# A Fourier convolution beside an FFN: the last inverse stage as even and odd parts in time

## The chip, the cores and the metric

The kernel runs on one core of a Trainium2 chip. The metric is the time that the device takes for one execution, in microseconds, as the median of several runs. The engines that matter are TensorE (PE in the profile, with its weight loads as PEld), VectorE (DVE), ScalarE (ACT), GpSimd (POOL), and SyncE (SP), which issues most of the DMAs. ACT issues a few DMAs too.

## The reference

The output is a token plus the product of two branches, both fed by the layer norm of the token: a state space layer, which is a causal convolution over time with a kernel of 2048 taps for each of 512 channels, and the SiLU of a SwiGLU feed-forward network (FFN).

```python
def _A_ref(u, A_re, A_im, B_re, B_im, C_re, C_im, log_dt, Dskip):      # L, D, N = 2048, 512, 128
    dt = jnp.exp(log_dt)[:, None]
    logdA, dB = dt * (A_re + 1j * A_im), dt * (B_re + 1j * B_im)
    P = jnp.exp(logdA[:, :, None] * l[None, None, :])
    K = jnp.einsum("dn,dnl,dn->dl", C_re + 1j * C_im, P, dB).real      # the 2048 taps
    ...                                # zero padding to 2L, rfft of K and u, product, irfft, first L
    return y + u * Dskip
def _B_ref(x, w_gate, w_up, w_down):                                   # F = 1792
    return (_silu(x @ w_gate) * (x @ w_up)) @ w_down

x = A_u                                                                # (1, 2048, 512), f32
xn = _layernorm(x, axis=-1)
return x + _A_ref(xn, ...) * _silu(_B_ref(xn, B_w_gate, B_w_up, B_w_down))
```

## The kernel before

Time is cut as 64 x 32: t = 32 t1 + t2. The 16 token tiles (j = 0 to 15) hold 128 tokens each: the 64 rows t1 of column t2 = 16 + j in the upper half of the partitions and those of its mirror 16 - j in the lower half (`rows`). Two neighbouring tiles make one of the eight blocks b of the FFN, each of which is worked in seven chunks c of its width: 24 matmuls for the gate, 24 for the up weights (line 717, called a half unit each below), and the down product (760; 769 for the last tile, in two halves of the channels). All weights and activations of the FFN are split into a high and a low f16 part, and three products of the parts are summed.

The convolution is a Fourier transform in two stages each way. The first stage on the tokens (`x_stage1`, line 568) transforms over t1: for each tile, six f16 matmuls of 64 rows by 128 columns, one for either half, in two row groups of the PE array at a time. ACT and DVE form the sum and the difference of the two halves and SP writes them to `ax_d` in DRAM. The taps are computed and transformed by `kg_tables` to `kg_s1` (lines 1106 to 1229) and go to `ak_d`. The second stage (`s2_mm`, 1267 for the taps and 1275 for the tokens) transforms over t2, `s2_prod` multiplies, and `s2_inv` (1320, with an ACT copy at 1330 and a DVE add and subtract at 1328 and 1329) goes back over the first digit of the frequency and writes `bs_d`. This is done for two halves of the channels, c = 0 and 1, of 256 each.

`final` does the last inverse stage. For a pair of tiles and a half of the channels (14 units; the last two tiles are done one by one over all channels, line 1372) it loads 512 KB of `bs_d` into `bt`, and four f32 matmuls (line 1365) take the 128 rows, real and imaginary parts of 64 frequencies, to 64 values of time: a 128x64 table for 16 + j and one for 16 - j, side by side in two column groups. DVE multiplies by the gate `zgs` (or by what was stored in `zg_d` and loaded again) at 1393, POOL or DVE adds the token (1396, 1398), which is loaded once more (1351), and the result is stored (1400; 1384 for the last tiles), one half by SP and one by ACT.

The kernel is written as tasks with an engine, buffers and dependences. Their order is a list written out as numbers (`LIST`), the place of each SBUF buffer another (`PLACES`); PSUM banks (eight, `p`) are given out in that order. `Plan.run` replays the list with priced durations only to choose the banks and to find gaps of PE that are filled with idle matmuls (line 1487). Each engine works its queue in order, and so does SP with its DMAs.

Of the kernel before, what the change touches and what calls it, by code (L numbers as in the profile page):

```python
# [26 lines left out]
NC = 7  # L27
# [11 lines left out]
BN = 2 * P + 6  # L39
# [7 lines left out]
    "###&#%#)#'#(#*#L#P#M#Q#S#N#+#l#O#K#W#X#$#J#`#g#I#Z#A#n#o#H#_#b#a#,#m#R#p#Y#/#h#|#i#q#U#c#[#B&0#]&2#.#^&5#V#T#t#v"  # L47
    "#j#u#{#r#D&A&6#w(2(3#9#s#}#d&B#k#x#2(4(5#y$#$$&1$,#5#e&;#f$%(7(8(9&<#@$'(6$|$}$&#1$+$-#E$((:(;(<(D(F&C&D#4$6$)$."
    "$/%##7%$%+(E(G$2&3$7(J(L(=$8%,$9#8%<#;$A&H(>(K$:$B$C$D#3$0$1$;&E(?(@#F$E&7$F$3&J$H(P#0$*#=$W$I&9&=&>(H&@$M$G(i#:"
    "$L&8$5$4%=%>$=(Q(V(W(X$N$O(A#-#z#?&F$b(M$J#>$P(B%%$Q#6$<(R&M&4(k$X(Y(c$S$T(C$p(I(d$R(Z(o&G%*%3$Y%4&:$>$?%&$K(S(j"  # L50
    "(l%'$Z$[(p(q(r&I&P$U%7$]#<(m(u$@$V$c&N(T$^({(|(v&K([%(%-&L%)%0(w$_$d&Q(x#C%?%@(U$g(]$e&_(_$f(^$`%.(n%5&R),(`(y$a"
    "$q%/&O%2$m$h(z%1%F%G$r$i%H$n$o%I$j)&)()')-))(a(b&i%8$k(s$l(}%J)#)$%A%B&S%9).)*)+)2)3):)%);$s$t$y(e)G)H)I)P%K%L%M"
    "$z${$u)Q%N&j$v$w$x)R%C&T&U&V&W%6%D%O&`&a&k%Q&s&t%E)S&u%R%P)<)=-Y)D-Z-_%:(N)T(f(g(t(O)E(h&b)>)?%;%S%T)F)J&w&?)K)U"
    "&x&y&m&n&v&o&q&p&z&X&Y&Z-`&c)]&d&e&f&l)^)L-[&[&^&r-]-a-^-o-v-s&{&])@)l)s)t)M)A-w)_)u)`&g)B)/)0)v&|)1-q-r)N)g)O.0"
    ".7-b)C.8-p-t-y-u-d-f-e-x-i&h-z.$-j-c-h)}*#*$*%.#.')h)i-k)j#G)k)V)X-l.1.:.H.G)W.I.J-g-m-n.*.+)Y.9.;.,-{..)Z)[.%.&"
    ".).--|)m.K.L)4.2.3.(-}.5)o.M.N.4.6.O.P)n.U.V)p.W.Y.X./.<.=.>)6.[.R)5.e)q)r.Q.x.].^)7)a.k)b)8.l.T.`.S.c)9)c.y/5.d"
    ".g)w/6/7._*;)d*<.f)x.b.a.Z.h)e.r.s)f.t.v/4.?.B.u.A.@.C.D.E/&)y/$/(*&*'*.*//%/'.m)z%U.z/8.o.q*=*D.n.p.w.|/#.{.}%V"
    ".i.F/9/:/;/B%]%^%s%t.j/)/</**E*L/+*>){)|/,%n%o%p/0%u*M*N///-/./1%[*0/?*O/A/=*1*8/2*9*:%q%r/D/I/F/>/@/C/E/3*?*@*A"
    "/H%e%f/L/Q/S%v%w&.*B/W/J/K'%*F*G*2*4%Z*3*5/N/M/O'$*H&}*I/_%X/e/n%W*C/P*(**/G*)/R/T*6/X%Y%_'+%`%b*7%a*+*,/Y/U*P*Q"
    "*R%c%x%i*-*V*W/V/[/^*J*K/f*S*_*`')/`/l%d/}/Z/]0#/a/b*T%y*r/m'('-*a/|*c'M0$/c*U'9/g/h*b%z/i%{%|*X/o0%/p0&0'/j'&/d"  # L60
    "/k/q/r*d'''#'**Z*e'/*Y','.*g'0'C/s/t*f/u*[*]%}&#&$&('1'2*^%g':';'<0D*y'N/w/v%j%k'D/x/y%h&,*z'E'O/z&%&)+&*h*o*p'3"
    "'4/{'='>'G'H'?'A'Q'R&&+''@%l*q+.&*'5'7%m050<'6&+&'0M'I'J'S'T0=060?&/+/+0&-'8+10>0708090(0@01*s'L*i*t'K0;0:0*0+0)"
    "*u0i0R0Q0-*v'U0/00020j0E*j0n0,0.030o0p'V+2+3+4*k0K0L0X0Y+5+6+70H040l0A0F0J0[0k0m0q0r0G0N+(+*0B*l0O0Z*{*m0C0I0]+)"
    "'Y0s0S0U0t*}0P*n0T0V++0W'Z0u0^*w*x+8+9*|+#+,+-0}'a0{1&0x0|0z1#0v0w1$+$+%0y+S+Z+[1(1)0_151*1'1-1B0`1<1C1.'o+:1=1/"
    "+c101+11+;1,0a0d1%12160b0c0e0f0g191;1?1718+@1Z0h1[1]'X1Y1>1:+<+=1F1H+d1314+A1^1_1`1@+B+D1I+>+?+k1J1L1D1E1G1A1K1M"
    "1N+C+E1a+F1e1h1i'['W'`'e'B']'b1b+H+I'^+G+l1j'P1c1d'_'c'd+P'p((()'F+T1g1o+Q+R1f1k(*1O1P+m1}1l+n'q'y'z'{(,1Q1U(-+U"
    "(.1m(/(11n1T's'f'g(0't'u'w'v'x1u1v1w20+V+W1R1S1V1p+o1q2#1W1x1s1y1r1t+p+q1X+r2+2-+X+Y2&2/2G2F+J1z1{2('}1|(#($(&(%"
    "(''i+L'j'k'l+K28'n+M2H+]2$2%2''m212)2:2*2,2223252I+_+^+`+s+t262729+a+N2J2K2L2M2O2P+b2Q24+O2T+e+f2N2R2S+g+h2U2W2Z"
    "2b2_2.2;2V2<2X2[+u2=2a+i+v2j2c2e(+2d2f2]2^2`+w+x+y2n+j2Y2k2s2u2w2p2l2m2o2g2q7a2{2h2x3#3$4T+z3&2r'|2y2z34352t364/"
    "2}3%333'374.2|+},#,$,&,%'r'h,*3839,'+{2i+|,(,)2>2?2A2B2@2C7b2v3(3:4-3)3*40414243453;3{3}3|47,+4#4$464%44,4484&4)"  # L70
    "2E,;,<4'4(2D493+3>4*4,3@4G3/3,4+3.3-303C3E7O,=3A,>3B3D3<3=,C3?7N4:4A4D4E4>4q4?4V,D,K,23F32313G3N3O,L4B3V4F4;4<3H"
    "3K3P3R4@,,3M3I3J3L3Q,33W4C3^3_3a,53`3b3Z3X3Y3[3]4|3S5#3d3m,-3e,.,63o3k3h4=5H3j3T3U3f4I4W3l3n3g3i4X4Y,M,74U4Z,/,8"
    ",94^4[4]4_3c3p3q3r,0,14a4J4L4K4o4r4t4H4s4p5J3s5K,:3u3t3v5=5M5$3w3x4M4P5I4}4`5%4Q5&4O4N4R,?,@5N5L5O,N4S7k,A5R5;3z"
    ",B3y5<,O7j5Q5P7|4u4v4x4w,E4y4z5'5+5(,F4b5S4c5*4l5)694{5,5-5>6.,T4d4m4e4i4f4g,U6-5@5A5?4j4k5E5D5B,]5C5.554n585652"
    "53,G,H5/504h5o546x,I5T5F6:595:,P,J515G5U5V,Q,R5W5X,S6;,^,_5]5^5_5`5a5b5Y6=6>5Z6<6?,`6A6@5q5s6z6{5r6|6/6B,e6D6C7}"
    "62,a5[606163655p5t646668675u5x5w5v5y5z,V6y6}7#7&7$,X7%8I,W,Y,b575d6E6S7(6F6G7*,Z6I6J6O5c,o,v,c,[,d6R6L,w5e5f5g6P"
    "6T6U6V7)6M7',f6H7+7,5h5k5l5i6K-#5j5m,m5n7Y6W6Z-$-+6X6Y7P7-7.6_7V6N7Z6[6Q6^6]7X7M70717/727473-%-&867[,n7W5{6$6*6%"
    "7{5|5}6`7`7]7^6a6c6b6+7r6#6'6(6),g,h7Q7R7S8R7U6d6e,x7_6f6h6g75797:6&7?7@7u7v7T7i-,-.8d8c7<7=7>7677--7;6j6i6k6u6o"
    "6v7A,z7G85,i8Q-/,y8.6l7w,{78,|6,7t6r7D7s,j,k,p,r-'6p7x7E6m6s,q,s6n,t,l-46w6t,u6q8m7C-5-67y,}-7-8-9878X8[8^7d7m7F"
    "-:-;8)8b8e8g8#7B7H8=8H8]8F8k8O8G-(8f-)-*8?-08+8z8n-<-=->-@-1-28%8h8*7I7J8$-3848&8(-?-A-B8o8l8/80888i8,8Z898:8S8T"  # L80
    "8p-C8Y8_8-817z8P8j9#7c8J8A8@8K8L8>8U8a8'7l-D-E-F8|7L-J8N-L-N-P-R8y8;-G-T7e7f-I7h-V8q8r828s8t-K8M8{837g8B8C8D-H8W"
    "8<8E7n7o7p8V-M-O8u8v-Q8x-X9(9)-S9*9+-U-W8`8}9$7q8w7K9%9&9'"
# [298 lines left out]
def kernel(  # L381
# [24 lines left out]
    bs_d = dram.tile([2, 16, BN, HD], F32, name="bs_d")  # L406
# [1128 lines left out]
```

## Time and profile before

| | us |
|---|---|
| median of 3 runs (lowest, highest) | 577.08 (577.01, 577.15) |
| the profiled execution | 578.55 |
| its span, first to last instruction | 576.8 |
| PE busy | 565.2 (98%) |
| DVE, ACT, POOL busy | 440.9, 334.7, 327.1 |
| matmuls of the FFN, lines 717, 760, 769, busy | 309.1, 143.2, 9.3 |
| line 1365, line 568, busy | 13.9, 11.9 |

Rows of the profile name line, engine, operation, written and read tiles, partitions x elements, and the number of records. An f32 matmul leaves two. "<-" behind an idle time names what released the engine. SPq and ACTq are the two queues of issued DMAs; their times are those of the issue. Busy times of matmuls overlap, so a sum of them is more than the stream's length; the chain's pieces don't overlap.

### The profile page before, as it was taken

What the parts mean: (1) busy time and instruction counts of PE and PEld (TensorE: products, weight loads), DVE (VectorE), ACT (ScalarE), POOL (GpSimd) and SP (SyncE); (2) the same over time, 40 slices, a digit from 0 to 9 for tenths busy, and PEclk for the clock granted to TensorE, in tenths of its full rate; (3) what the DMA queues carried; (4) which work ended last, traced back from release to release, by engine and by line L of the source; (5) the groups of instructions that cost most, each with busy time, mean ns of one, the idle gap of its engine ahead of it and who ended that gap; (6) DMA issues with size and microseconds to landing.
All of it is one profiled execution on the core that took longest, in us unless ns stands there. A gap on an engine that the chain in (4) does not pass through costs nothing.

```text
span 576.8 us, 18270 instructions
## 1 busy us (share of the span) xinstructions
PE 565.2 (98%) x7570; PEld 405.9 (70%) x7570; DVE 440.9 (76%) x1006; ACT 334.7 (58%) x686; POOL 327.1 (57%) x301
## 2 busy tenths in 40 slices
PE   7999999999999999999999999999999999999996
PEld 3788896564886588757867688765766674678765
DVE  5988889846788998988887899977978765643533
ACT  5988667646767266777777778746752323231111
POOL 0144352299998168629998789997516152520041
PEclk9999999999999999999999999999999999999999
DMA  8888722251003171058005452697879987998997
GB/s 249 237 260 265 225 74 74 49 174 67 29 2 85 29 174 47 2 110 275 22 1 126 97 149 74 149 212 181 270 230 248 287 281 218 258 306 234 233 256 203
DMA packets 113155, 93.17 MB, mean 162 GB/s; under 512 B 51184, under 2 KB 97648, under 8 KB 113072
## 3 DMA queue, kind: packets, MB, share of 16 engines
q1 hardware_dynamic: 110432, 89.61, 55.5%
q10 hardware_dynamic: 2640, 2.39, 1.5%
q8 instruction: 59, 0.97, 0.7%
q14 instruction: 24, 0.20, 0.1%
HBM read 55.94 MB, written 32.90 MB: 154 GB/s over the span
## 4 chain that ended last, share of the span: by engine, by line
PE 93%; DMA 2%; SPq 2%; DVE 1%; issue 1%; ACT 0%; DVEq 0%
PE p L717 50%; PE p L760 24%; PE p L1181 5%; PE p L1267 3%; PE p L568 2%; PE p L1275 2%; PE p L1365 2%; PE p L1320 2%; PE p L769 2%; PE p L1214 2%; DMA arena<-bs_d 1%; DMA arena<-in_A_u_dram 1%; SPq L464 1%; PE p L830 1%; SPq L485 1%
## 5 line engine op out<-in xcount | busy, mean ns | idle before, releaser
L717 PE MATMUL p<-arena,wu 128*128 128x256 f16 x1344 | 154.6, 273 | 0.0
L717 PE MATMUL p<-arena,wg 128*128 128x256 f16 x1344 | 154.5, 273 | 0.0
L717 PEld LDWEIGHTS <-wg 128*128 128x128 f16 x1344 | 130.5, 98 | 21.4 <-issue 2.8
L717 PEld LDWEIGHTS <-wu 128*128 128x128 f16 x1344 | 130.2, 98 | 20.2 <-issue 3.7
L760 PE MATMUL p<-wd,arena 128*128 128x512 f16 x630 | 143.2, 379 | 0.0
L760 PEld LDWEIGHTS <-arena 128*128 128x128 f16 x630 | 59.7, 98 | 71.8 <-issue 6.1
L1114 POOL TENSOR_TENSOR arena<-arena 128x1536 f32<-128x1536 f32 x32 | 90.6, 2839 | 22.0 <-DVE arena L850 8.3
L739 ACT ACTIVATE arena<-p,inv 128x512 f32<-128x512 f32 x56 | 37.7, 685 | 65.9 <-PE p L717 62.5
L741 DVE SCALAR_TENSOR_TENSOR p<-p,shc,arena 128x512 f32<-128x512 f32 x56 | 42.0, 756 | 41.9 <-PE p L717 33.3
L1106 POOL TENSOR_TENSOR arena<-arena 128x1024 int32<-128x1024 int32 x32 | 62.4, 1955 | 20.0 <-DVE arena L532 7.8
L743 ACT CAST arena<-p 128x512 f16<-128x512 f32 x56 | 32.6, 586 | 38.4 <-DVE p L741 31.9
L1149 DVE TENSOR_TENSOR arena<-arena,p 128x512 f32<-128x512 f32 x64 | 43.6, 681 | 6.3 <-POOL arena L1047 2.5
L1129 ACT ACTIVATE p<-arena 128x512 f32<-128x512 int32 x64 | 38.5, 606 | 12.9 <-POOL arena L1106 8.3
L1396 POOL TENSOR_TENSOR arena<-arena 128x512 f32<-128x512 f32 x12 | 15.0, 1269 | 49.3 <-DMA arena<-in_A_u_dram 21.6
L1130 ACT ACTIVATE p<-p,halfpi 128x512 f32<-128x512 f32 x64 | 41.9, 662 | 1.2
L744 DVE TENSOR_TENSOR arena<-p,arena 128x512 f16<-128x512 f32 x56 | 37.5, 683 | 6.0 <-ACT arena L743 5.9
L1131 ACT ACTIVATE p<-arena 128x512 f32<-128x512 int32 x64 | 38.0, 604 | 6.9 <-POOL arena L1106 4.2
L1298 POOL TENSOR_TENSOR arena<-arena 128x512 f32<-128x512 f32 x16 | 20.3, 1274 | 30.7 <-DVE arena L1295 26.2
L1297 POOL TENSOR_TENSOR arena<-arena 128x512 f32<-128x512 f32 x16 | 20.4, 1276 | 25.4 <-issue 15.0
L1181 PEld LDWEIGHTS p<-arena 128*32 128x32 f32 x2048 | 29.4, 110 | 5.4 <-issue 2.9
L1181 PE MATMUL p<-arena 128*32 128x64 f32 x2048 | 32.3, 220 | 0.0
L1293 DVE TENSOR_TENSOR arena<-p,arena 128x512 f32<-128x512 f32 x32 | 21.1, 685 | 13.9 <-PE p L1275 7.7
(198 smaller groups left out, 815.5 us busy)
## 6 DMA issues: line engine op xcount, KB each, us to landing
ax_d<-arena SPq DMA_DIRECT2D x32, 256.0 KB, 2.9
ak_d<-arena SPq DMA_DIRECT2D x16, 512.0 KB, 5.6
arena<-ak_d SPq DMA_DIRECT2D x16, 512.0 KB, 4.6
arena<-ax_d SPq DMA_DIRECT2D x16, 512.0 KB, 5.1
bs_d<-arena SPq DMA_DIRECT2D x32, 256.0 KB, 3.8
arena<-in_A_u_dram SPq DMA_DIRECT2D x62, 128.0 KB, 3.9
arena<-in_B_w_down_dram SPq DMA_DIRECT2D x14, 512.0 KB, 5.1
arena<-bs_d SPq DMA_DIRECT2D x12, 512.0 KB, 6.7
```

The source lines that it names most:

```text
L717: T.matmul(pg.t[:, i * 256:(i + 1) * 256].rearrange("p (a t) -> p a t", a=2), w[:, wl, d, i * P:(i + 1) * P], x[:, :, xl, d, :], start=(k ...
L739: add("ACT", 0.69, lambda: S.activation(sg.f32(), pg.t, AF.Silu, scale=inv[:, c, 0:1]), rd=[pg], wr=[sg], c=1, pr=e)
L741: add("DVE", 0.75, lambda: V.scalar_tensor_tensor(pu.t, pu.t, shc[:, c:c + 1], sg.f32(), op0=ALU.mult, op1=ALU.mult), rd=[sg], wr=[pu], c= ...
L744: add("DVE", 0.7, lambda: V.tensor_tensor(hh.view(F16)[:, 512:1024], pu.t, hh.view(F16)[:, 0:512], op=ALU.subtract), rd=[pu], wr=[hh], c=1 ...
L760: T.matmul(z.t, h[:, hl, i * 256 + t * P:i * 256 + (t + 1) * P], w[:, wl, i], start=(c == 0 and i == 0 and k == 0), stop=(c == NC - 1 and ...
L1106: G.tensor_tensor(a, h_[:, :, :, None].to_broadcast([P, 2 * GT, 4, 8]), l_[:, :, None, :].to_broadcast([P, 2 * GT, 4, 8]), op=ALU.add)
L1114: G.tensor_tensor(e, p_[:, :, :, None].to_broadcast([P, 3 * GT, 4, 8]), q_[:, :, None, :].to_broadcast([P, 3 * GT, 4, 8]), op=ALU.mult)
L1129: add("ACT", 0.62, lambda: S.activation(tc_.t, a(), AF.Abs, scale=SIN_SCALE), rd=[an], wr=[tc_], pr=pr)
L1130: add("ACT", 0.7, lambda: S.activation(tc_.t, tc_.t, AF.Sin, bias=halfpi, scale=-1.0), rd=[key("ones")], wr=[tc_], c=4, pr=pr)
L1131: add("ACT", 0.62, lambda: S.activation(ts.t, a(), AF.Sin, scale=SIN_SCALE), rd=[an], wr=[ts], pr=pr + 0.2)
L1149: V.tensor_tensor(o[:, :, 0:64].rearrange("p d (s j) -> p d s j", s=2), e[:, :, 0:64].rearrange("p d (s j) -> p d s j", s=2), t[:, :, None ...
L1181: T.matmul(kt[h * 32:(h + 1) * 32, (r * GD + dd) // 4], o[:, ri, dd + h, 64:96], o[:, ri, dd + h, 0:64], start=(ri == 0), stop=(ri == 1), ...
```

## The change

Each token tile now holds a half of time of two mirrored columns instead of all of time: tile 2b the 32 rows t1 = 32 to 63 of the columns 16 + 2b, 17 + 2b and of their mirrors, tile 2b + 1 the rows 31 down to 0 of the same columns.

`final` handles a block b, a pair of tiles. A table of 64x32 takes the real parts to the part that is even about the middle of time, another takes the imaginary parts to the odd part: eight matmuls for a unit, in two row groups and four column groups, into two banks (`pc`, `ps`). ACT copies the odd part (a new line, 1399), DVE adds for one half of time and subtracts for the other (1402, 1403), and the product with the gate follows from SBUF. The last pair is done like the others, over both halves of the channels. Since one half of time is read and written backwards, a pair's token loads and stores are four DMAs where they were two.

`x_stage1` handles a pair: 24 matmuls of 32 rows by 128 columns, in four row groups, where two tiles had 12 of 64 rows. The table `f1x` is twice as wide. The first scaling of the gate weights is published before its reciprocal is computed. `bs_d` loses its padding rows. `LIST` and `PLACES` are new throughout.

```diff
     def x_stage1(...)
-        for k, (wl, xl) in enumerate(((0, 0), (0, 1), (1, 0))):
-            for h in range(2):
-                r = slice(h * 64, h * 64 + 64)
-                T.matmul(pa[h].t, (f1x_t if j or not h else f1yb.view(F16))[r, wl * P:(wl + 1) * P], x.view(F16)[r, xl * 512:(xl + 1) * 512],
-                         start=(k == 0), stop=(k == 2))
+        for a in range(2) if half is None else (half,):
+            for k, (wl, xl) in enumerate(((0, 0), (0, 1), (1, 0))):
+                for g in range(4):
+                    r = slice(g * 32, g * 32 + 32)
+                    T.matmul(pa[at[g]].t, w[r, a, wl], x[a].view(F16)[r, xl * 512:(xl + 1) * 512],
+                             start=(k == a == 0), stop=(k == 2 and a == 1), tile_position=(g * 32, 0))
...
     def final(...)
-        add("SP", 0.6, lambda h=h: sy.dma_start(vw(fx)[h * 64:(h + 1) * 64], rows(xv, h, j0, nj)[:, :, cs]), up=[fx], pr=pr, dma=0.72, root=True)
+        for k in range(2):
+            for h in range(2):
+                add("SP", 0.6, lambda h=h, k=k: sy.dma_start(two(fx[k].f32(), h), rows(xv, h, j0 + k)[:, :, cs]), up=[fx[k]], pr=pr,
+                    dma=0.36 * nd / HD, root=True)
...
-            for i in range(nj):
-                for h in range(2):
-                    T.matmul(py.t[h * 64:(h + 1) * 64, i * nd:(i + 1) * nd], j2_t[:, h * 64:(h + 1) * 64], b[:, 2 * i + h], start=True, stop=True,
-                             tile_position=(0, h * 64))
+                for g, (m, i) in enumerate(at):
+                    for ri, t in enumerate((pc.t, ps.t)):
+                        r = slice(ri * 64, ri * 64 + 64)
+                        T.matmul(t[g * 32:(g + 1) * 32, q], j2_t[r, m * 32:(m + 1) * 32], v[r, 2 * i + m], start=True, stop=True, tile_position=(ri * 64, g * 32))
+            add("ACT", 0.38, lambda q=q, o=ov2: S.copy(o(1), ps.t[:, q]), rd=[key(f"py{tag}{h}")], up=[ps], wr=[ot], c=1, pr=pr)
+            def both(q=q, o=ov2):
+                V.tensor_tensor(o(0), pc.t[:, q], o(1), op=ALU.add)
+                V.tensor_tensor(o(1), pc.t[:, q], o(1), op=ALU.subtract)
...
-        for h in range(2):
-            add(("SP", "ACT")[h], 0.62, lambda h=h: (sy, nc.scalar)[h].dma_start(rows(ov, h, j0, nj)[:, :, cs], vw(ot)[h * 64:(h + 1) * 64]), ...
+            for m in range(2):
+                add(("SP", "ACT")[m], 0.62, lambda m=m, k=k, o=o: (sy, nc.scalar)[m].dma_start(rows(ov, m, j0 + k)[:, :, cs], two(o(), m)), ...
```

The order moves in three places that the prediction speaks of. On SP, at the start, the queue's first DMAs, before (`in_A_u` are the tokens, `in_B_w_gate` and `in_B_w_up` the weights, `f1x` the first stage's table):

```order
L485 DMA arena<-in_A_u_dram 64x512 x2
L464 DMA wd<-in_B_w_gate_dram 128x4x256
L485 DMA arena<-in_A_u_dram 64x512 x3
L464 DMA f1x_t<-in_f1x_dram 128x256
L485 DMA arena<-in_A_u_dram 64x512
L464 DMA wd<-in_B_w_up_dram 128x4x256 x2
```

And now:

```order
L493 DMA arena<-in_A_u_dram 64x1x512 x6
L472 DMA wd<-in_B_w_gate_dram 128x4x256
L472 DMA arena<-in_f1x_dram 128x512
L472 DMA wd<-in_B_w_up_dram 128x4x256
L472 DMA wd<-in_B_w_gate_dram 128x4x256
```

All six token loads stand ahead of the first gate weights, and the table behind them.

On ACT, from the square of the first gate weights (615, then 634) to the high part of the first up weights (687, then 713), before:

```order
L615 ACTIVATE wg,ssq<-wd 128x1024
L530 ACTIVATE arena<-arena,mv 128x512
L531 ACTIVATE arena<-arena,rstd 128x512
L530 ACTIVATE arena<-arena,mv 128x512 x2
L615 ACTIVATE wu,ssq<-wd 128x1024
L531 ACTIVATE arena<-arena,rstd 128x512
L615 ACTIVATE wu,ssq<-wd 128x1024
L531 ACTIVATE arena<-arena,rstd 128x512
L575 COPY arena<-p_101 128x512
L678 ACTIVATE wg<-wd,scw 128x4x128 x2
```

And now:

```order
L634 ACTIVATE wg,ssq<-wd 128x1024
L538 ACTIVATE arena<-arena,mv 128x512
L539 ACTIVATE arena<-arena,rstd 128x512 x2
L634 ACTIVATE wu,ssq<-wd 128x1024
L704 ACTIVATE wg<-wd,scw 128x4x128 x2
L634 ACTIVATE wg,ssq<-wd 128x1024
L634 ACTIVATE wu,ssq<-wd 128x1024
L592 COPY arena<-p_103 128x512
```

The split of the first gate weights (678, then 704) comes after two squares instead of three and ahead of the first stage's copies.

On DVE, the last steps of the kernel, before (1393 and 1381 multiply by the gate from PSUM, 1382 adds the token):

```order
L1393 TENSOR_TENSOR arena<-p_106,arena 128x512
L1393 TENSOR_TENSOR arena<-p_103,arena 128x512
L1381 TENSOR_TENSOR arena<-p_99,arena 128x256
L1382 TENSOR_TENSOR arena<-arena 128x256
L1381 TENSOR_TENSOR arena<-p_101,arena 128x256
```

And now (1402 and 1403 add and subtract the parts, 1423 and 1411 multiply by the gate, 1412 adds the token):

```order
L1403 TENSOR_TENSOR arena<-p_99,arena 128x256
L1423 TENSOR_TENSOR arena<-arena 128x512
L1402 TENSOR_TENSOR arena<-p_103,arena 128x256
L1403 TENSOR_TENSOR arena<-p_103,arena 128x256
L1411 TENSOR_TENSOR arena<-arena 128x256
L1412 TENSOR_TENSOR arena<-arena 128x256
```

The gate's product no longer reads PSUM, so nothing of TensorE's last inverse stage is left for DVE to wait for at the end; on PE the last instructions are now those of the down product (769, then 795), where two matmuls of line 1372 followed them.

More of the change, by code (lines that the diff above doesn't have):

```diff
@@ L484, in rows_in @@
             eng, q = ("ACT", nc.scalar) if j < 2 and h else ("SP", sy)
-            add(eng, 0.6, lambda h=h, q=q: q.dma_start(b.f32(512)[h * 64:(h + 1) * 64], rows(xv, h, j)[:, 0]), up=[b], rd=rd, pr=pr,
-                dma=dma_us(131072, 64), root=True)
+            add(eng, 0.6, lambda h=h, q=q: q.dma_start(two(b.f32(512), h), rows(xv, h, j)), up=[b], rd=rd, pr=pr,
+                dma=0.85 if j == 1 else dma_us(131072, 64), root=True)
     xt, xT = {}, {}
@@ L602, in w_load @@
             k = ND
-        load(lambda: b.f32().rearrange("p (a f) -> p a f", a=k), src, [b], 524288, 128 * k, pr, ahead=30.0 if again else None)
+        load(lambda: b.f32().rearrange("p (a f) -> p a f", a=k), src, [b], 760000 if nm == "g" and c == 0 else 524288, 128 * k, pr, ahead=30.0 if again else None)
     def w_norm(nm, c):
@@ L1333, in s2_inv, with final @@
                 rd=[b], up=[key(f"bs{c}")], c=0, dma=0.9)
-    def final(js, cs, c):
-        nj, nd = len(js), cs.stop - cs.start
-        j0 = js[0]
-        pr = W["o0"] + W["oc"] * c + W["o1"] * (j0 // 2) + (5 if nd == D and j0 % 2 else 0)
+    def final(b, cs, c):
+        nd = cs.stop - cs.start
+        j0 = 2 * b
+        pr = W["o0"] + W["oc"] * c + W["o1"] * b
         tag = f"{j0}_{c}"
-        ready = [key(f"bs{h}") for h in range(2) if cs.start < (h + 1) * HD and cs.stop > h * HD]
-        vw = lambda b: b.f32().rearrange("p (j d) -> p j d", j=nj)
-        bt = buf(f"bt{tag}", 4096, "bt", int(W["c_bt"] + 0.5))
+        at = places(b)
@@ L1399, in final @@
-        for h in range(2):
-            add(("SP", "ACT")[h], 0.62, lambda h=h: (sy, nc.scalar)[h].dma_start(rows(ov, h, j0, nj)[:, :, cs], vw(ot)[h * 64:(h + 1) * 64]), rd=[ot], up=[key("out")], c=0,
-                dma=dma_us(131072, 64 * nj), pr=e)
+            bt = bts[h] = buf(f"bt{tag}{h}" if b == NB - 1 else f"bt{tag}", 4096, "bt", int(W["c_bt"] + 0.5))
+            for first, lo, n in ((0, 0, 1), (33, 1, 1), (2, 2, 2)) if b == 0 else ((2 * j0, 0, 4),):
+                load(lambda h=h, bt=bt, lo=lo, n=n: bt.f32().rearrange("p (s d) -> p s d", d=HD)[:, lo:lo + n], bs_rows(h, 0, first, ((32, 2), (64, 64), (1, n))),
+                     [bt], 131072 * n, 128, pr, rd=[key(f"bs{h}")])
@@ new lines, in final @@
+        ot = ots[c]
+        for k in range(2):
+            if b < ZK and k:
+                break
+            o = (lambda: ot.f32()) if b < ZK else (lambda k=k: ot.f32()[:, k * HD:(k + 1) * HD])
+            zz = (lambda: z.f32()) if b < ZK else (lambda k=k: zgs[j0 + k].f32()[:, cs])
+            add("DVE", 0.7 if b < ZK else 0.42, lambda o=o, zz=zz: V.tensor_tensor(o(), o(), zz(), op=ALU.mult), rd=[z if b < ZK else zgs[j0 + k]],
+                wr=[ot], c=1, pr=pr, port=True)
+        for k in range(2):
+            o = lambda k=k: ot.f32()[:, k * HD:(k + 1) * HD]
+            y = key(f"oo{tag}{k}")
+            if b < 6:
+                add("POOL", 0.66, lambda k=k, o=o: G.tensor_tensor(o(), o(), fx[k].f32(), op=ALU.add), rd=[fx[k]], up=[ot], wr=[y], c=1, pr=pr)
+            else:
+                add("DVE", 0.42, lambda k=k, o=o: V.tensor_tensor(o(), o(), fx[k].f32(), op=ALU.add), rd=[fx[k]], up=[ot], wr=[y], c=1, pr=pr, port=True)
+            for m in range(2):
+                add(("SP", "ACT")[m], 0.62, lambda m=m, k=k, o=o: (sy, nc.scalar)[m].dma_start(rows(ov, m, j0 + k)[:, :, cs], two(o(), m)), rd=[y], up=[ot, key("out")], c=0,
+                    dma=dma_us(65536, 64), pr=pr)
@@ L1447 @@
         prep(hf)
[L1448 to L1449 removed]
+    for b in range(2):
+        x_stage1(b)
     for j0 in range(4, NTT, 4):
```

290 lines of the change are left out of this document (146 added, 144 removed).

## The prediction

> **What bounds the kernel now.** I read the page from the top: busy time by engine, the slices, the chain that ended last; then the chain in order of time for the two places that the change edits, and at last the start and the end of the timeline.
>
> ```profile
> span 576.8 us, 18270 instructions
> PE 565.2 (98%) x7570; PEld 405.9 (70%) x7570; DVE 440.9 (76%) x1006; ACT 334.7 (58%) x686; POOL 327.1 (57%) x301
> DMA  8888722251003171058005452697879987998997
> PE 93%; DMA 2%; SPq 2%; DVE 1%; issue 1%; ACT 0%; DVEq 0%
> ```
>
> TensorE is busy for 98% and carries 93% of the chain, so a microsecond of matmul taken out of the stream is worth nearly a microsecond, until something else ends last. The DMA slices name the candidate: from slice 30 on they stand at 7 to 9. The forecast is a sum over TensorE's stream, plus what the start, the end and the transfers add or take back.
>
> **Term 1, the last inverse stage.** Line 1365 (and 1372 for the last two tiles) multiplies a 128x64 table by 256 columns, two such tiles side by side.
>
> ```profile
> 493.12 1.01 PE p L1365 x8
> 507.85 1.01 PE p L1365 x8
> 535.27 5.40 PE L1365 MATMUL p<-arena,j_t 128*64 128x256 f32 x48
> 540.61 2.79 PE L717 MATMUL p<-arena,wu 128*128 128x256 f16 x24
> 551.16 0.65 PE L1372 MATMUL p<-arena,j_t 128*64 128x256 f32 x4
> 553.38 1.95 PE L1365 MATMUL p<-arena,j_t 128*64 128x256 f32 x16 [0.38 <-DMA arena<-bs_d]
> 557.85 4.06 PE L760 MATMUL p<-wd,arena 128*128 128x512 f16 x18
> 571.01 0.65 PE L1372 MATMUL p<-arena,j_t 128*64 128x256 f32 x4
> ```
>
> An f32 matmul leaves two records, so one unit of four matmuls is x8. Three units stand alone (the first and the last are shown), 3 x 1.01 = 3.03 us. Six in a row take 540.61 - 535.27 = 5.34, which is 0.89 each. The third place lasts 557.85 - 551.16 = 6.69, less the wait of 0.38. Together 14.7 us lie ahead of the last FFN matmul.
>
> The new unit is eight matmuls of 64x32, two row groups by four column groups. That shape runs in this kernel already, on line 1267:
>
> ```profile
> 461.60 2.87 PE p L1267 x96
> 484.69 1.02 PE p L1267 x32
> ```
>
> From 32 to 96 records adds 1.85 us, so 16 records cost 0.46 and a place costs 1.02 - 0.92 = 0.10 once. The new order has 16 units at seven places: 16 x 0.46 + 7 x 0.10 = 8.1 us. Term 1 is -6.6. The lower bound of a unit is four slots become two, 0.89 / 2 = 0.445, which makes the term -6.9. An upper bound with only two tiles at once would be 16 x 1.78, but the L1267 row has the same tile and excludes it.
>
> The unit adds an ACT copy and a DVE add and subtract, and holds two PSUM banks where it held one. The rows are L1330 and L1328, which do the same for the stage before:
>
> ```profile
> L1330 ACT COPY arena<-p 128x256 f32<-128x256 f32 x32 | 10.4, 388 | 21.2 <-PE p L1320 16.3 <-DMA arena<-zg_d 4.9
> L1328 DVE TENSOR_TENSOR arena<-p,arena 128x256 f32<-128x256 f32 x32 | 13.3, 417 | 8.4 <-ACT arena L1330 8.4
> 500.00:520.00 20.00, 20.00 (x302) 14.69 (x301) 10.65 (x24) 6.28 (x16) 3.78 (x3) 1.00 1.02 290
> 520.00:540.00 20.00, 20.00 (x173) 15.57 (x173) 8.23 (x17) 3.13 (x5) 1.26 (x1) 1.00 0.87 224
> 540.00:560.00 20.00, 19.62 (x154) 13.63 (x150) 10.42 (x17) 2.44 (x4) 5.94 (x5) 1.00 0.99 254
> 560.00:577.00 17.00, 11.66 (x97) 9.10 (x95) 5.09 (x10) 1.90 (x4) 5.21 (x5) 0.98 0.72 211
> ```
>
> (Windows: length, then PE, PEld, DVE, ACT and POOL busy with counts, clock, DMA share, GB/s.) 16 x 0.39 = 6.2 us on ACT and 32 x 0.42 = 13.4 on DVE fall where ACT was busy for 14 of 77 us and DVE for 34: hidden. The cover fails where units stand in a row. Four units take eight banks and 1.85 us of PE; the first pair of banks is free 0.39 + 0.83 us after its unit ends, at about 1.7. That just fits, so a row of units can cost the FFN matmul behind it some tenths.
>
> **Term 2, the tokens' first stage.** Line 568 had 6 matmuls of 64x128 a tile; now 24 of 32x128 serve two tiles, four row groups at a time. The columns streamed are the same.
>
> ```profile
> 15.28 0.75 PE p L568 x6
> 118.48 2.69 PE p L568 x24
> 330.35 0.75 PE p L568 x6
> 331.11 1.05 PE p L1214 x32
> 391.11 0.64 PE p L1275 x32
> ```
>
> One tile costs 0.75; three more add 1.94, so a round of two concurrent matmuls is 0.216 us and a place costs 0.10. Sixteen tiles at nine places are 16 x 3 x 0.216 + 9 x 0.10 = 11.3 us. If four groups run as freely, eight pairs of six rounds at nine places give the same: 0. The rows with four row groups are dearer to enter: L1214 has four rounds in 1.05, L1275 two in 0.64; 0.205 a round and 0.23 a place. With 48 rounds of 0.216 and nine places of 0.23 the stage costs 12.4. Nearest is L1214, whose loads have 64 columns; its 0.24 a round (1.05 less a place of 0.10, by four) gives 48 x 0.24 + 0.9 = 12.3. I take that, +1.0, with the ends 0 and +2.8 (below).
>
> **Term 3, the start.** On SP the first gate weights now stand behind six token loads, where they stood behind two.
>
> ```profile
> 2.25 0.59 SPq L464 DMA_DIRECT2D wd<-in_B_w_gate_dram  x1
> 9.18 1.06 ACT L615 ACTIVATE wg<-wd 128x1024 bf16<-128x1024 f32 x1 [1.86 <-DMA wd<-in_B_w_gate_dram]
> 10.41 0.69 DVE L499 BATCH_NORM_STATS2 st<-arena 128x6 f32<-128x512 f32 x1 [1.61 <-DMA arena<-in_A_u_dram]
> 15.25 1.41 DVE L532 SCALAR_TENSOR_TENSOR arena<-arena,rstd 128x512 f16<-128x512 f32 x2
> 16.64 1.41 DVE L547 COPY arena<-p 128x512 f16<-128x512 f16 x4
> 17.01 1.34 ACT L678 ACTIVATE wg<-wd,scw 128x512 f16<-128x512 f32 x2
> 18.53 2.79 PE L717 MATMUL p<-arena,wg 128*128 128x256 f16 x24
> 22.48 2.79 PE L717 MATMUL p<-arena,wu 128*128 128x256 f16 x24
> ```
>
> The gate landed at 9.18 and the third token tile at 10.41. In the new order tokens land first and the gate about then, at 10 (bounds 9.2 and 11.4, one microsecond after 10.41). I follow both kernels to the first matmul with the up weights, at 22.48 now: both have done four token tiles and half an FFN unit by then. DVE no longer idles 1.61 us for the third tile, so its residuals start that much earlier, at about 12.4 instead of 14.1. Four residuals at 0.71, four copies at 0.35 and the small steps between end at 17.0; the gate's low half follows. The half unit then runs from about 17.2 to 19.9, and the second token pair, 1.4 us, to 21.3. I take 21.7, since ACT's new row has its own waits: -0.8. The gate at 9.2 with nothing else behind it gives -1.9, at 11.4 +0.6. ACT's table load, which stood ahead of the tokens, now waits for the first of them; the step after it waits for DVE's square root anyway, which covers it.
>
> **Term 4, the end.** The final half unit, with its add and subtract, moves ahead of the last FFN matmuls.
>
> ```profile
> 571.12 0.47 ACT L781 ACTIVATE arena<-p,zsc 128x256 f32<-128x256 f32 x1 [2.26 <-PE p L769]
> 571.78 0.42 DVE L1381 TENSOR_TENSOR arena<-p,arena 128x256 f32<-128x256 f32 x1 [2.00 <-PE p L1372]
> 572.73 0.49 SPq L1384 DMA_DIRECT2D out_dram<-arena  x1
> ```
>
> DVE waited for L1372; now it waits for ACT alone, done at 571.59: -0.1. The multiply, the add, the store and its landing stay.
>
> **Term 5, the transfers.** Bytes stay; the number of DMAs grows, since a reversed half of time can't share one with its mirror: 28 more loads of tokens, 28 more stores (half on SP), two fewer table loads, so 40 more on SP.
>
> ```profile
> 518.67 1.29 SPq L1351 DMA_DIRECT2D arena<-in_A_u_dram  x2
> SPq L1351 <- DVE arena L1393: 5.0, 1, 5.0
> SPq L1332 <- DVE arena L1328: 5.3, 2, 2.9
> ```
>
> At 0.65 each that is 26 us on SP. Between 480 and 577 SP issued 89 DMAs, some 55 us at 0.62, and waited in order for the rest; the two longest entries of those waits are shown. So SP goes to 81 of about 90 us. I add +0.5, mostly from tiles landing later than a unit wants them; the list's whole order is also new, which can remove waits like the 0.38 above or bring more, +-1.5.
>
> Sum: -6.6 + 1.0 - 0.8 - 0.1 + 0.5 = -6.0 us. The profiled execution took 578.55, 1.75 outside the span; the median of the runs is 577.08, 0.3 over the span. The new span should be 570.8 and the median 571.1.
>
> **The rivals.**
>
> A, the four row groups do not overlap. If each load of 128 columns costs what a load and its matmul cost in the transposes, the stage is bound by loads:
>
> ```profile
> 17.20 0.55 PE p L541 x8
> ```
>
> 0.55 / 8 = 0.069 each; 192 of them and nine places give 14.1, +2.8 in place of +1.0: 572.9. Against it: L1267 loads and starts a tile every 32 ns, though of 32 columns. The Trainium skill ("TensorE: Matmul & The Clock Gate", Part 3, Measured speedup vs the span model) gives 3.07x, not 4x, for four row tiles at 512 columns; as an estimate 192 x 0.216 / 3.07 + 0.9 = 14.4, the same side. For two groups the row disagrees: 0.647 for six matmuls of 0.216 is 2.0x once they run in a row. No run here shows four at 512 columns.
>
> B, the transfers keep the end where it is. The share of the last four windows is 69.8 us of 77, and bytes don't change. If 0.96, the mean of the three full windows, is a ceiling, the stage shrinks by 4.3, not 6.6: 573.4. If nothing at all can start earlier, all of Term 1 goes: about 577.7, no change. Against it: the slices before 480 leave room for tokens to be fetched earlier.
>
> C, slower: SP, issuing in order. With 81 us of issue, waits above 97 - 81 = 16 us make the stage longer than today, and it waits for some 40 now. Most of these are slack that a fuller queue eats; if 22 of them are real, the last units' loads come 6 us late and PE waits for them, so that Term 1's gain isn't seen: 583. For it speaks that a wait of 5.0 on line 1351 holds back every load behind it; against it, that PE waited only 0.38 for a load from bs_d in the last stage.
>
> D, the start turns late and new waits appear, with Terms 1 and 2 as forecast: +3 to +6, 574 to 577.
>
> **How the numbers follow.** Forecast 0.56; A 0.13; B 0.16, a third of it at no change; C 0.08; D 0.07, half of it at no change. A measurement of this kernel tells 0.2%, 1.15 us, from no change. Faster: 0.56 + 0.13 + 0.11 + 0.03 = 0.83; within it 0.05 + 0.04 = 0.09; slower, C, 0.08. The range starts where Term 1 is -6.9, Term 2 is 0, Term 3 -1.9 and the waits -0.7, at 567.5, and goes up over A and most of B to 576.0, leaving out about 0.05 below and 0.15 above.
>
> **What would show it.** Term 1: the line of the new stage sums to about 8 us, eight tiles starting within some ns. Term 2: 24 records in 1.3 to 1.5 us, against 1.75 for A. Term 3: the first up-weight matmul at 21.7. Term 4: the last add waits for ACT. Term 5: SP waits in the last stage well below 16 us. PE idle time over 3 us after 480, released by a DMA, would make me wrong through B or C; any stall of PE between 23 and 60 us through D.

## The result and the profile after: 47% slower

The changed kernel takes 850.32 us as the median of four runs (849.58 to 850.67), the kernel before 577.05 beside it: a ratio of 1.4734, 95% interval 1.4708 to 1.4759. The prediction said 571.1, within 567.5 to 576.0. It was wrong by 279 us and on the wrong side.

The page of the changed kernel, the lines that answer to those shown of before: span, busy time, then the slices of PE, of the granted clock and of the DMA engines, and the chain that ended last.

```profile
span 848.5 us, 18892 instructions
PE 593.7 (70%) x7797; PEld 410.3 (48%) x7797; DVE 453.4 (53%) x1040; ACT 340.2 (40%) x702; POOL 327.8 (39%) x313
PE   5699899999999699989989999395042503231230
PEclk8899999999999799999989999698567665575575
DMA  2776525202041470325568695531231111112111
PE 46%; DMA 26%; SPq 20%; issue 3%; DVE 2%; ACT 2%; POOL 0%; ACTq 0%; DVEq 0%; POOLq 0%
```

PE's busy time grew little (565.2 before), but PE is busy for 70% of the span and not for 98%. It idles in the first slices and in the last third. In that last third the DMA engines stand mostly at 1 to 3 tenths: transfers lead the list of what PE waits for, while most of the transfer engines have nothing to do. SP's issuing, 2% of the chain before, is 20% now.

The windows say it sharply. (Columns as in the prediction's windows; the last three are clock, DMA share and GB/s. The first two rows are the start, the others lie in the last stage.)

```profile
5.00:10.00 5.00, 2.81 (x13) 1.00 (x11) 0.88 (x3) 0.91 (x1) 0.00 (x0) 1.00 0.13 51
10.00:15.00 5.00, 0.00 (x0) 0.10 (x1) 1.97 (x9) 1.82 (x3) 0.53 (x1) 0.71 0.13 51
640.00:660.00 20.00, 2.44 (x23) 1.94 (x20) 3.32 (x7) 1.18 (x2) 1.45 (x2) 0.67 0.13 51
687.00:707.00 20.00, 0.00 (x0) 0.00 (x0) 1.70 (x4) 0.00 (x0) 2.76 (x4) 0.50 0.13 52
820.00:848.00 28.00, 0.00 (x0) 0.00 (x0) 1.70 (x4) 1.15 (x3) 0.00 (x0) 0.50 0.13 45
```

A share of 0.13, again and again, is 2/16, and the rate is 45 to 52 GB/s. The kernel before, at the start:

```profile
5.00:10.00 5.00, 4.87 (x23) 1.97 (x21) 3.28 (x17) 2.26 (x3) 0.52 (x1) 1.00 1.07 285
```

The packets of the trace tell whether two engines work all the time or sixteen now and then. Between 640 and 660 us exactly two packets are under way for 92% of the time; in the kernel before (540 to 560) it is most often 16 or 17. A packet takes 46 ns at the median in both, and its median size is 1 KB in both. So an engine is as fast as ever, and two of them work. SP's queue at the start (start, length, line, what is moved):

```profile
0.73 12.57 SPq L493 DMA_DIRECT2D arena<-in_A_u_dram  x6
13.35 2.46 SPq L472 DMA_DIRECT2D wd<-in_B_w_gate_dram  x1
```

And in the last stage:

```profile
654.14 10.37 SPq L1378 DMA_DIRECT2D arena<-in_A_u_dram  x1
664.56 4.91 SPq L472 DMA_DIRECT2D arena<-zg_d  x1
```

The token loads took some 0.6 us each to issue before; these six take 12.6 together. The first three still take 0.5 to 0.7, the next three 2.8, 4.9 and 2.8: the issue itself is held up once earlier loads are under way. The longest takes 10.4 (3.2 in the kernel before), and SP issues nothing else meanwhile. The waits of PE that lead the list (in total, times, longest) are for the loads of `bs_d`, line 1395, and for ACT behind them:

```profile
PE p L1395 <- DMA arena<-bs_d: 98.6, 6, 25.5
PE p L1395 <- ACT arena L765: 33.6, 1, 33.6
```

What the four kinds of transfer have in common is how their address pattern in DRAM begins. Token loads and stores now take two columns of time, each with 32 rows, as the front part tells. The loads of `bs_d` were turned as well, which its diff does not show:

```diff
-                load(..., bs_rows(h, 0, first, ((BN, 16), (32, 8), (1, n))), ...
+                load(..., bs_rows(h, 0, first, ((32, 2), (64, 64), (1, n))), ...
```

Real parts and imaginary parts come first, so the slowest dimension has 2 entries where it had 16. For the tokens it went from 64 rows to 2 columns. The experiments take that as theory 1: a DMA runs on as many engines as its slowest dimension allows. The rival, theory 2, was the prediction's own case C: more DMAs on SP, and a new list.

### The profile page after: what moved, and what is told of

The parts are those of the page before. It is cut to its first block, busy times and chain, and to the rows that moved or that the text cites. A ratio compares the mean times of both kernels' runs of the same rounds, so it can differ in the third digit from the quotient of the medians.

```text
span 848.5 us, 18892 instructions
## 1 busy us (share of the span) xinstructions
PE 593.7 (70%) x7797; PEld 410.3 (48%) x7797; DVE 453.4 (53%) x1040; ACT 340.2 (40%) x702; POOL 327.8 (39%) x313
## 4 chain that ended last, share of the span: by engine, by line
PE 46%; DMA 26%; SPq 20%; issue 3%; DVE 2%; ACT 2%; POOL 0%; ACTq 0%; DVEq 0%; POOLq 0%
PE p L743 24%; DMA arena<-in_A_u_dram 13%; PE p L786 12%; SPq L1378 8%; SPq L472 7%; DMA out_dram<-arena 4%; DMA arena<-zg_d 3%; PE p L1207 3%; DMA bs_d<-arena 3%; SPq L1433 2%; SPq L493 2%; PE p L1293 1%; PE p L580 1%; PE p L1346 1%; DMA arena<-ax_d 1%
## 5 line engine op out<-in xcount | busy, mean ns | idle before, releaser
L743 PE MATMUL p<-arena,wg 128*128 128x256 f16 x1344 | 160.6, 278 | 3.9 <-ACT arena L765 3.1
L743 PE MATMUL p<-arena,wu 128*128 128x256 f16 x1344 | 157.4, 275 | 3.8 <-DVE arena L1183 2.0
L786 PE MATMUL p<-wd,arena 128*128 128x512 f16 x630 | 151.4, 394 | 0.0
L743 PEld LDWEIGHTS <-wg 128*128 128x128 f16 x1344 | 132.8, 100 | 29.4 <-issue 8.2
L1395 PE MATMUL p<-arena,j_t 64*32 64x256 f32 x256 | 16.9, 584 | 158.9 <-DMA arena<-bs_d 98.6
L1429 POOL TENSOR_TENSOR arena<-arena 128x256 f32<-128x256 f32 x24 | 17.0, 724 | 248.9 <-DVE arena L1423 154.1
L1395 PEld LDWEIGHTS p<-arena,j_t 64*32 64x32 f32 x256 | 5.5, 142 | 167.6 <-issue 52.9
L1402 DVE TENSOR_TENSOR arena<-p,arena 128x256 f32<-128x256 f32 x16 | 6.7, 421 | 81.2 <-ACT arena L1399 81.2
L1399 ACT COPY arena<-p 128x256 f32<-128x256 f32 x16 | 5.8, 374 | 110.6 <-PE p L1395 43.9
L1175 DVE TENSOR_TENSOR arena<-arena,p 128x512 f32<-128x512 f32 x64 | 43.7, 683 | 10.4 <-POOL arena L1140 4.9
L507 DVE BATCH_NORM_STATS2 st<-arena 128x6 f32<-128x512 f32 x16 | 11.1, 691 | 47.3 <-DMA arena<-in_A_u_dram 47.3
```

The costliest lines, as they stand in the source:

```text
L743: T.matmul(pg.t[:, i * 256:(i + 1) * 256].rearrange("p (a t) -> p a t", a=2), w[:, wl, d, i * P:(i + 1) * P], x[:, :, xl, d, :], start=(k ...
L786: T.matmul(z.t, h[:, hl, i * 256 + t * P:i * 256 + (t + 1) * P], w[:, wl, i], start=(c == 0 and i == 0 and k == 0), stop=(c == NC - 1 and ...
L1175: V.tensor_tensor(o[:, :, 0:64].rearrange("p d (s j) -> p d s j", s=2), e[:, :, 0:64].rearrange("p d (s j) -> p d s j", s=2), t[:, :, None ...
```

## The experiments

**One: only the addresses put back.** The changed kernel, its list, its number of DMAs, its bytes and its pieces, with 64 or 128 rows first; which rows land where is then not the reference's:

```diff
     def rows(v, h, j):
-        b, k = divmod(j, 2)
-        ...
-        return v.rearrange("s j d -> j s d")
+        t2 = 16 + j if h == 0 else 16 - j if j else 0
+        return v[:, t2:t2 + 1]
...
-                     ... bs_rows(h, 0, first, ((32, 2), (64, 64), (1, n))),
+                     ... bs_rows(h, 0, first, ((32, P), (1, n))),
```

> The changed kernel with nothing altered but the addresses in DRAM of four kinds of transfer: token loads and stores take 64 rows of one column (64x512 or 64x256) where they took 2 columns x 32 rows, and the loads of bs_d take 128 rows in one dimension where they took 2 x 64. Number of DMAs, bytes and piece lengths stay; which rows land where is not the reference's. Theory 1 (a DMA whose slowest dimension in DRAM has 2 entries runs on 2 of the 16 DMA engines): every stall goes, token loads at the start land at over 200 GB/s instead of 51, and the time is what the sum of the prediction said, 571 (567 to 577). Theory 2 (more DMAs on SP, which issues in order, and the new list's waits): the DMAs and the order are the same, so 800 to 850 stays. Theory 3 (both): between 600 and 800.

Measured: 580.3 us, ratio 1.0055 (1.0035 to 1.0075). The start, its windows and SP's first row:

```profile
5.00:10.00 5.00, 5.00 (x23) 2.11 (x22) 4.47 (x19) 3.63 (x6) 0.53 (x1) 1.00 0.92 270
```

```profile
0.74 4.06 SPq L491 DMA_DIRECT2D arena<-in_A_u_dram  x6
```

270 of the 273 us are gone with nothing altered but the shape of the address patterns of four kinds of transfer, so theory 2 can't be their cause. But the 571 of the prediction is not reached either; the last three experiments are about those 9 us.

**Two to four: the kernel before, with 2, 4 and 8 entries first.** Its list and counts stay; the patterns turn, and `bs_d` loses its padding rows.

```diff
     def rows(v, h, j0, nj=1):
-        ...
+        ns = 64 * nj // K
+        g, r = divmod(j0 // nj, 64 // ns)
+        c0 = (16 if h == 0 else 0) + g * K
+        return v[r * ns:(r + 1) * ns, c0:c0 + K].rearrange("s j d -> j s d")
...
-                     ... bs_rows(h, 0, first, ((BN, 16), (32, 8), (1, n))),
+                     ... bs_rows(h, 0, first, ((32, K), (32 * K, 128 // K), (1, n))),
```

> The kernel before with the same four kinds of transfer (token loads, loads of bs_d, stores of the output) turned to 2 x rows: the same number of DMAs, the same bytes, the same list of tasks, but 2 entries in the slowest dimension in DRAM. Which rows land where is not the reference's; bs_d loses its padding rows. Theory 1: the last stage has 8.2 MB of bs_d, 4.2 of tokens and 4.2 of output, 16.6 MB at 51 GB/s = 325 us where PE has about 100 of work, and the start is some 15 us later: 577 + 225 + 15 = about 815 (760 to 880). Theory 2: 577 to 585, since neither the count of DMAs nor the order changes.

> As before_outer2, with 4 entries in the slowest dimension (4 columns x fewer rows; 4 x 32 rows of bs_d). Theory 1 (engines in use = entries of the slowest dimension): 102 GB/s, 16.6 MB take 163 us where PE has 100: 640 (610 to 680), and DMA share 0.25 where only these run. A rival (a fixed cost of each such DMA, not its engines): the same time as with 2. Theory 2: 577 to 585.

> As before_outer2, with 8 entries. Theory 1: 204 GB/s, 16.6 MB take 81 us, less than PE's work there, but the transfers with 16 engines share the first 8: 577 to 600. A fixed cost of each such DMA: as with 2.

Measured: 864.6 with 2 entries (one run), 681.2 with 4 (one run), 599.5 with 8 (ratio 1.0407, 1.0364 to 1.045), against 577.2. One window from the last stage of each, with 2 entries:

```profile
720.00:740.00 20.00, 0.00 (x0) 0.00 (x0) 0.76 (x1) 1.27 (x2) 0.00 (x0) 0.50 0.13 50
```

With 4:

```profile
640.00:660.00 20.00, 5.40 (x48) 4.58 (x47) 3.68 (x6) 0.47 (x1) 3.79 (x3) 0.73 0.27 98
```

With 8:

```profile
580.00:597.00 17.00, 9.23 (x84) 7.69 (x81) 4.60 (x10) 1.42 (x3) 2.49 (x2) 0.93 0.50 171
```

Shares of 0.13, 0.27 and 0.50 are close to 2, 4 and 8 engines of 16, and the rate rises with them: 50, 98, 171 GB/s. A fixed cost of each DMA would have given the three kernels one time. So the old kernel is made as slow as the new one by the shape alone, and the dose sets the effect. The sizes came out above the middle of what was expected (815, 640, 577 to 600), the first and third within their ranges and the second a microsecond beyond.

The Trainium skill has the rule ("DMA: Bandwidth & Descriptors", Why a DMA increments its semaphore by 16 and not by 1, "How many engines (k)"): a DMA is split over the largest number of engines up to 16 that divides the size of the slowest dimension of both of its patterns, and from SP and ACT over the lowest-numbered ones. These shares agree with it for 2, 4 and 8. That all of SP's and ACT's transfers of 2 entries fall on the same two engines agrees with the 0.13 that several DMAs in flight share.

**Five and six: a part of the repair at a time.** The patterns of experiment one, for the first stage's token loads alone, or for the last stage's token loads and stores alone:

```diff
-            ... q.dma_start(two(b.f32(512), h), rows(xv, h, j)) ...
+            ... q.dma_start(two(b.f32(512), h), rows64(xv, h, j)) ...
```

> The changed kernel with only the 32 token loads of the first stage (4.2 MB) taking 64 rows of one column, as in after_rows64; token loads and stores of the last stage and the loads of bs_d keep 2 entries in the slowest dimension. Rows of the tokens are not those of the reference. Two engines as the limit: PE lost 32 us up to 500 us of the changed kernel against the kernel before (461.5 against 493.9 busy), and that returns: 818 (800 to 835). If the first stage's loads were the main cause: below 700.

> The changed kernel with only the token loads and the stores of the last stage (8.4 MB together) taking 64 rows of one column. Which rows land where is not the reference's. Two engines as the limit: 8.4 MB less at 51 GB/s is 164 us: 690 (650 to 720). If the loads of bs_d alone set the pace: 830 to 850.

**Seven: the loads of `bs_d` alone,** with real and imaginary parts as two DMAs of 64 rows:

```diff
-                     ... bs_rows(h, 0, first, ((32, 2), (64, 64), (1, n))),
+                     ... [bs_rows(h, 0, first + 32 * i, ((64, 64), (1, n))) for i in range(2)] ...
```

> The changed kernel with each load of bs_d as two DMAs of 64 rows each (real and imaginary parts apart), 20 more DMAs on SP, nothing left out. Two engines as the limit: 8.4 MB less at 51 GB/s is 164 us: 690 (650 to 720). If the number of DMAs on SP sets the pace: 850 to 870.

Measured, one run each: 806.1, 752.4 and 719.2. That is 44, 98 and 131 us less than 850.3, 273 together, where experiment one took 270: the three parts add up to the whole. The first and the third time lie within the expected ranges (the third at its upper edge), the second doesn't: the token loads and stores of the last stage gave 98 where 164 less was the estimate. All 21 MB at 51 GB/s are 411 us, and 270 was lost, so by this estimate a third of the slow transfer time lay beside other work; how much of it in each part was not measured by itself. None of the parts is "the" cause, and 20 more DMAs on SP in experiment seven did not keep it from gaining 131.

**Eight: a whole kernel that keeps the change.** A reversed half of time with its rows first would need a slowest dimension that steps backwards, which no DMA of these kernels has; so its two columns stay first, and POOL issues those DMAs. The ascending half goes by column, and the loads of `bs_d` as in experiment seven:

```diff
+    def tin(h, k, dst, src):
+        if k:
+            return G.dma_start(dst(slice(h * 64, h * 64 + 64)), src)
+        for i in range(2):
+            sy.dma_start(dst(slice(h * 64 + i * 32, h * 64 + i * 32 + 32)), src[i])
```

> The whole computation, nothing left out: loads of bs_d as in split_bt; token loads and stores of the ascending half of time as two DMAs of 32 rows each; those of the reversed half, which need the column as the slowest dimension, issued by POOL instead of SP and ACT. If POOL's DMAs with 2 entries spread over more engines in turn than SP's: 580 to 620, POOL's in-order queue being the new wait. If they too use the same two engines: 6.3 MB at 51 GB/s, 4.2 of them in the last stage, 82 us beside 100 of PE: 600 to 680.

Measured: 651.7, ratio 1.128 (1.1247 to 1.132). Better than 850 and still far from 577. POOL's queue at the start (its own instructions; line 417 is a DMA):

```profile
1.29 0.81 POOL L417 DMA_DIRECT2D arena<-in_A_u_dram  x1 [0.84 <-POOLq L1569]
10.32 0.52 POOL L495 MEMSET dsk<- 128x512 f32 x1 [8.22 <-DVE rstd L542]
10.79 0.68 POOL L417 DMA_DIRECT2D arena<-in_A_u_dram  x1
19.62 1.30 POOL L417 DMA_DIRECT2D arena<-in_A_u_dram  x2 [8.16 <-DVE rstd L542]
```

The second half tile is asked for at 10.79, behind a memset that waits 8.22 us for DVE: a load behind compute in an in-order queue. POOL's DMAs, all with 2 entries first, have a DMA queue of their own. Between 600 and 650 us the packets of that queue (`q0`, software_dynamic) took 21.7% of the 16 engines' time, more than the 12.5% of two engines, so POOL's narrow DMAs did use more than two. The time is outside the 580 to 620 expected for that case all the same; how much of the rest is POOL's queue was not separated. None of these kernels computes everything and beats the kernel before.

**Nine to eleven: the 9 us that the shape doesn't explain.** First the kernel before with nothing but the change's number of DMAs:

```diff
-            add("SP", 0.6, lambda h=h: sy.dma_start(vw(fx)[h * 64:(h + 1) * 64], rows(xv, h, j0, nj)[:, :, cs]), ...
+            add("SP", 0.6, lambda h=h: [sy.dma_start(vw(fx)[h * 64:(h + 1) * 64, i], rows(xv, h, j0, nj)[:, i, cs]) for i in range(nj)], ...
```

(and the stores alike).

> The kernel before with only the number of DMAs of the change: each token load and store of the last stage that held two columns is two DMAs of 64 rows of one column, 28 more loads and 28 more stores, 42 of them on SP; nothing left out, all on 64 rows. The prediction's fifth term says +0.5, 577.7 (576 to 579). If SP's in-order issue is what the changed order ran into (a stall of 4.4 us of PE in after_rows64 and a slower clock behind it): 580 to 586. It is no test of the two engines.

Then experiment one with fewer DMAs, first the loads, then the stores as well:

```diff
-                add("SP", 0.6, lambda h=h, k=k: sy.dma_start(two(fx[k].f32(), h), rows(xv, h, j0 + k)[:, :, cs]), ...
+                add("SP", 0.6, lambda h=h, k=k: sy.dma_start(fx[k].f32(), rows128(xv, j0 + k)[:, cs]) if h == 0 else None, ...
```

> after_rows64 (580.3) with the token loads of the last stage as one DMA of 128 rows where there were two of 64: 30 fewer DMAs on SP, the same bytes. Which rows land where is not the reference's. If SP's in-order issue held the tail (fx landing late, POOL's add late, ACT's stores in its queue ahead of the copies of the odd part): 572 to 575. If the rest comes from the list's order alone: 579 to 581.

> rows64_fx1 with the stores merged too: one store of 128 rows, the first half of time by SP and the second by ACT, where each half had one on either; 16 fewer on SP and 16 fewer on ACT. Not the reference's rows. SP's and ACT's in-order issue as the cause of the rest: 570 to 573, what the prediction's first four terms give. Otherwise as rows64_fx1.

Measured: 587.9 for the kernel before with 56 more DMAs, ratio 1.0162 (1.0131 to 1.0193), which is 9.4 us (the medians lie 10.3 apart); 578.0 for the merged loads, ratio 0.9996 (0.9977 to 1.0015); 572.5 for merged loads and stores, ratio 0.9901 (0.9876 to 0.9926). PE's longest wait in the kernel before with more DMAs:

```profile
PE p L1372 <- DVE arena L1381: 6.4, 1, 6.4
```

What held it, from that kernel's chain (line 1400 is a store, 781 ACT's step from the down product to the gate, 1381 the multiply by it):

```profile
574.55 0.61 ACTq L1400
575.25 1.92 DMA out_dram<-arena
577.17 0.47 ACT arena L781
577.66 0.43 DVE arena L1381
```

ACT's stores stand in its queue ahead of that step. PE's longest wait in experiment one:

```profile
PE p L1393 <- ACT arena L1397: 4.4, 1, 4.4
```

With the loads merged (an execution of 579.5 us, above the median):

```profile
PE p L1396 <- ACT arena L1400: 3.3, 1, 3.3
```

With loads and stores merged no wait of PE for another engine or a DMA in the last stage is on its list, and the chain by engine reads:

```profile
PE 96%; DVE 2%; DMA 1%; issue 1%; ACT 0%; DVEq 0%
```

How the wait of 4.4 comes about, in the timeline of experiment one (line 1376 is a token load, 1427 POOL's add, 1431 a store, 1397 ACT's copy of the odd part, which frees a PSUM bank):

```profile
556.42 4.29 ACTq L1431 DMA_DIRECT2D out_dram<-arena  x5
556.79 0.65 SPq L1376 DMA_DIRECT2D arena<-in_A_u_dram  x1
558.33 0.72 POOL L1427 TENSOR_TENSOR arena<-arena 128x256 f32<-128x256 f32 x1 [4.49 <-DMA out_dram<-arena]
560.80 0.65 ACT L1397 COPY arena<-p 128x256 f32<-128x256 f32 x2 [3.88 <-DMA out_dram<-arena]
561.23 1.10 PE L1393 MATMUL p<-arena,j_t 64*32 64x256 f32 x14 [4.37 <-ACT arena L1397]
562.26 4.98 PE L784 MATMUL p<-wd,arena 128*128 128x512 f16 x12
```

ACT issues stores in order with its copies, a store waits for its add, and the matmuls need the copy. The page puts ACT's idle time down to a store. The twelve matmuls of line 784 behind the wait then take 4.98 where the same twelve took 2.76 elsewhere in this trace (541.47): the granted clock was 0.55 there (562.3 to 567.3) against 1.00, so the wait costs its length and some 2.2 us more. Merging the loads alone left 3.3 of it; merging the stores as well took it away. So the stores are shown to hold it, and the expectation that SP's loads alone would free it was wrong (572 to 575 expected, 578.0 measured). SP's stores and ACT's were merged together, so that it is ACT's queue and not SP's is read from the timeline and not shown by a run.

## Why the prediction was wrong, point by point

**The step that failed** is the sentence "Bytes stay; the number of DMAs grows" in Term 5, and with it the landing at 10 us in Term 3 and the missing loads of `bs_d` in Term 1. I priced the turned transfers by their number and their issue on SP and took their rate from the kernel before. The code states the shape of each, and the shape set the rate: 51 GB/s in place of up to 351 (10 to 15 us of the kernel before). The loads of `bs_d` I counted only as a cover of Term 1, without reading their pattern. None of the rivals held this; B capped the end by the sum of all transfers at a share of 0.96, where the kernel fell to 0.13.

**Term 1, the last inverse stage, -6.6: right.** Its places in the chain, in order of time, of the kernel with merged loads and stores:

```profile
483.00 0.43 PE p L1396 x16
488.17 0.59 PE p L1396 x16
516.80 1.89 PE p L1396 x64
531.89 1.46 PE p L1396 x48
541.94 1.02 PE p L1396 x32
546.31 1.02 PE p L1396 x32
556.60 1.11 PE p L1396 x32
558.15 0.66 PE p L1396 x14
```

They sum to 8.18 at eight places; 8.1 at seven was forecast. The row of line 1267, with its way to split a place's fixed part from its units, carried over.

**Term 2, the tokens' first stage, +1.0: too dear at the full clock.** Two pairs, in the same kernel's chain:

```profile
114.42 1.41 PE p L581 x24
121.11 1.41 PE p L581 x24
```

A pair is 1.41, inside the forecast 1.3 to 1.5, and so are all of the last seven; eight of them would be 11.3: nothing gained and nothing lost, the lower end. Four row groups at 512 columns do overlap, and rival A (1.75) is refuted. Six rounds in 1.41 are 0.235 each. A matmul of 512 columns on the whole array takes 0.216 in this chain (line 787, 24 in 5.18 at 105.13), and 24 x 0.216 / 1.41 makes the four groups 3.7 times as fast as one after another. The Trainium skill ("TensorE: Matmul & The Clock Gate", Part 3, Measured speedup vs the span model) gives 3.07x for four row tiles at 512 columns; this trace shows more. The first pair is worked in two halves at the start and took 2.64 here, at a granted clock of 0.53 (14 to 16 us); it belongs to Term 3.

**Term 3, the start, -0.8: lost to the shape, and not shown with wide loads.** The first matmul with the up weights, in the changed kernel:

```profile
38.88 0.61 PE L743 MATMUL p<-arena,wu 128*128 128x256 f16 x4
```

And in experiment one:

```profile
21.27 0.61 PE L741 MATMUL p<-arena,wu 128*128 128x256 f16 x4
```

In the kernel with merged loads and stores, whose start is the same:

```profile
22.36 0.61 PE L744 MATMUL p<-arena,wu 128*128 128x256 f16 x4
```

38.9 as changed, because six loads of 128 KB at 51 GB/s held the gate back. With wide loads ACT begins on the gate at 10.2, as forecast, but the matmul starts at 21.3 or 22.4, where 21.7 was forecast; and the start of the kernel before, 22.48 in its own trace, is at 21.51 in that of experiment nine. So one start differs by 1 us from execution to execution, as much as the term, and its gain is not shown. In the trace with 22.36 the idle matmuls end earlier, PE waits 1.5 us for DVE, and the clock behind that wait is 0.53 where experiment one has 1.00: this is rival D on a small scale.

**Term 4, the end, -0.1:** the last multiply waits for ACT alone, as said (0.44 and 1.08 in experiment one), and the term is too small to be told apart.

**Term 5, 40 more DMAs, +0.5: 9.4 in the kernel before.** That is the second error, and it stands without the first: with wide transfers the change would have come out at 580.3, slower than before and outside the range. The bound of +-1.5 was taken from the list's waits, and SP's 81 of 90 us were read as room. In both traces the price is seen where ACT's work on PSUM (781 there, 1397 here) stands behind its stores. Case C, with SP as the place and 583 as the time, was the nearest to it and was given 0.08.

The sum closes within 2 us: 577.2 - 6.6 (Term 1) + 0.0 (Term 2) - 1.2 (Term 3, from its trace) + 9.4 (Term 5) = 578.8 against 580.3 for the wide version. The 9.4 was measured in another kernel, at another wait, so this is an estimate and no proof. Where the DMAs are merged, 577.5 - 6.6 - 0.1 (Term 3, from its trace) = 570.8 stands against 572.5. What the last 2 us are stays open; that 572.5 lies near the forecast of 571.1 speaks for Term 1 and not for the forecast, which had these DMAs unmerged.

## What to carry to other kernels

When a change turns the layout of a tile, write down for every DMA that touches it the first dimension of its pattern in DRAM before pricing anything else: with 2 entries there, DMAs of 64 to 512 KB from SP and ACT ran at 51 GB/s together, on 2 of 16 engines. A DMA share that sat at 0.13, 0.27 or 0.50 while PE waited was a count of engines here, not a load. A DMA that is issued by a computing engine is an instruction in that engine's queue: count which copies stand behind each store.

## What the runs showed of the hardware that I had not expected

A DMA's issue is not a fixed cost: with narrow transfers under way one issue on SP lasted up to 10.4 us, against a median of 0.54 and at most 3.2 in the kernel before, and a wide one behind them was held as well (a load of `zg_d`, 128 rows first, took 4.91 to issue). And the granted clock of PE was lower at its waits, 0.50 in a window without matmuls (687 to 707), and still 0.55 in experiment one for the 5 us behind a wait of 4.4: the mean was 0.847 over the changed kernel and 0.994 in experiment one.
